# 384 rows of w_down on eight chosen DMA engines, in a decode kernel of cached attention and a SwiGLU block

## The chip, the cores and the metric

The kernel runs on one core of a Trainium2 chip. The metric is the device time of one execution in microseconds; lower is better. A core has a matrix engine (TensorE, PE in the profile), a vector engine (VectorE, DVE), a scalar engine (ScalarE, ACT), a general engine (GpSimd, POOL) and an engine that does little but issue DMAs (SyncE, SP). Sixteen DMA engines, numbered 0 to 15, move data between memory (HBM) and the on-chip buffer (SBUF, 128 partitions). A DMA that an engine issues is cut into shares for some of the sixteen; each DMA engine works off its shares in the order in which one issuing engine queued them.

## The reference

One token goes through an attention block with a long key/value cache and through a gated feed-forward block, and the two results are mixed by a sigmoid gate. With D = 512, 32 query heads, 8 key/value heads, a cache of 32768 rows of 128, and F = 1792:

```python
g = _sigmoid((x * gate_w).sum(-1, keepdims=True))
# A: attention with the cache, then the output matrix
q = (x @ wq).reshape(B, Sq, 32, 128).transpose(0, 2, 1, 3)
k, v = jnp.repeat(k_cache, 4, axis=1), jnp.repeat(v_cache, 4, axis=1)
p = _softmax(jnp.einsum("bhqd,bhkd->bhqk", q, k) * 128 ** -0.5, axis=-1)
a = jnp.einsum("bhqk,bhkd->bhqd", p, v).transpose(0, 2, 1, 3).reshape(B, Sq, 4096) @ wo
# B: feed-forward
b = (_silu(x @ w_gate) * (x @ w_up)) @ w_down
return g * a + (1 - g) * b
```

All tensors are bf16. The two caches are 64 MB each, wq and wo 4 MB each, w_gate, w_up and w_down 1.75 MB each: 148 MB are read for one small row of 512 outputs.

## The kernel before

SBUF holds five pages of 32 KB per partition (`page`, PG_A = 0, PG_B = 1, PG_C = 2, PG_V = 3 and 4). Weights, K and V go through these pages, so a load can be issued only when the page that it fills is free.

**SyncE's queue** sets the order of all large transfers. It issues, one after the other and each behind the wait that frees its page: wq (L335), w_gate and w_up (L337), K of group 0 (two pages, L315), then for each group g the K of g (L315 for g = 1, L306 after that) and the V of g - 1 (L330), the V of the last group, the first 1664 rows of w_down into the tile `wd` (L345), the last 128 rows of w_down (L351), and wo in five chunks (L356), of 16, 9, 4, 2 and 1 rows of each partition's 32.

In the main load of w_down a partition holds FM = 13 consecutive rows (13 KB), and FR = 1664 rows are covered. The other 128 rows go to the first 32 partitions of PG_A, four rows to a partition, in eight DMAs of four partitions each (`wx`). PG_A is free when TensorE has transposed the last K unit (`sem_fill` at UPG * G); wo is put into PG_V, which is free when the V of the group before the last has been used (`sem_v_free`).

**The start of the kernel** computes the queries from wq, then g and u of the feed-forward block. VectorE makes t = silu(g) * u * (1 - gate) as `trow`, four partitions' strips of 448 columns, and spreads it into `tmask` (L706, 1792 columns, each strip masked to its own partition). TensorE turns t into columns with matmuls against a column of ones (L541): 13 for the main rows into `tT`, 4 for the others into `tX` (copies at L713 and L714). Two matmuls then release the loop (L553).

**The loop** goes over the eight groups. TensorE transposes K in 16 units of eight blocks (`emit_fill`, L364, two bf16 at a time as one f32), VectorE copies each unit to SBUF (L735), TensorE multiplies with the queries (L376). Maxima, exponentials (ACT, L619) and sums follow, and the V of the group before is multiplied with its exponentials (L433). The third load of K (g = 2) is issued when half of group 1's units have been transposed.

**The end** (`emit_end`) uses the last V, adds up, and runs the strips of w_down: one matmul for each of `wd`'s 13 columns and four for `wx` (`emit_strip`, L232), all into the four rows of `ps_c`. It then multiplies with wo as chunk after chunk lands (L232 for the first, L243 for the others), and the row of 512 is stored in two halves (L267).

GpSimd fills constants at the start (L275 to L287) and afterwards only passes on semaphores of the K loads. It issues no DMA.

Of the kernel before, what the change touches and what calls it, by code (L numbers as in the profile page):

```python
# [6 lines left out]
ALU = mybir.AluOpType  # L7
# [5 lines left out]
def bass_gated_mix__gqa_block_cached__swiglu_ffn__decode_kernel(  # L13
# [62 lines left out]
    assert G % 2 == 0  # L76
    PAD = 768

    XQ, XE, FX = 8, 4, 4
    XP = XQ * XE  # L80
    FM = FC - XP * FX // 128
    FR = 128 * FM
    assert FR + XP * FX == F and FX == NSTRIP

    with ExitStack() as es:
        def S_(name):
            return es.enter_context(nc.semaphore(name))
# [9 lines left out]
        sem_ld_g = S_("s_ld_g")  # L97
        sem_ld_wd = S_("s_ld_wd")
        sem_ld_wx = S_("s_ld_wx")
        sem_ones = S_("s_ones")  # L100
        sem_dc = S_("s_dc")
        sem_pz = S_("s_pz")
# [59 lines left out]
        qblk = T("qblk", [128, (G + 2) * STEP], BF16)  # L162
        qcur = T("qcur", [128, 2, 2 * HPG], BF16)
        tT = T("tT", [128, FM], BF16)
        tX = T("tX", [XP, FX], BF16)
        pad = T("pad", [128, PAD // 2], BF16)
        page = T("page", [128, NPG, PAGE], BF16)
        wd = T("wd", [128, FM, NOUT], BF16)
# [13 lines left out]
        O2a = T("O2a", [128, WOJ], BF16)  # L182
        O2 = T("O2", [128, WOJ], BF16)
        res_row = T("res_row", [128, 128], BF16)

        def P(name, shape, dt):
            return es.enter_context(nc.psum_tensor(name, shape, dt))
# [34 lines left out]

        wq_v = page[:, PG_Q, 0 : KC * H * DH].rearrange("p (c n) -> p c n", c=KC)
        wgu = page[:, PG_F, 0 : 2 * KC * F].rearrange("p (w c f) -> p w c f", w=2, c=KC)
        wx = page[0:XP, PG_A, 0 : FX * NOUT]
        wx_v = wx.rearrange("p (i n) -> p i n", i=FX)
        wo_v = page[:, PG_X, 0 : WOJ * NOUT].rearrange("p (j n) -> p j n", j=WOJ)
        qall = qblk[:, :].rearrange("p (g e c) -> p g e c", e=2, c=2 * HPG)

# [42 lines left out]
        with nc.Block("main") as block:  # L272
            @block.gpsimd
            def _(pool):
                pool.memset(ones_f[:, :], 1.0).then_inc(sem_ones, 1)  # L275
                pool.memset(ones_bf[:, :], 1.0).then_inc(sem_ones, 1)
                pool.memset(r_row[:, 0, 0:1], 0.0).then_inc(sem_r, 1)
                n, k = 1, 1
                while n < 128:
                    pool.wait_ge(sem_r, k)  # L280
                    pool.tensor_scalar(
                        r_row[:, 0, n : 2 * n], r_row[:, 0, 0:n], float(n), None, op0=ALU.add
                    ).then_inc(sem_r, 1)
                    n *= 2
                    k += 1
                pool.wait_ge(sem_r, k)
                pool.tensor_scalar(  # L287
                    r_row[:, 1, :], r_row[:, 0, :], -1.0, None, op0=ALU.mult
                ).then_inc(sem_r, 1)
                for g in range(1, G):  # L290
                    pool.wait_ge(sem_k[1], 16 * g)
                    if g > 1:
                        pool.wait_ge(sem_k[0], 16 * (g + 1))
                    else:
                        pool.wait_ge(sem_k1, 16)
                    pool.sem_inc(sem_k[1], 16)

            @block.sync
            def _(sp):
                def load_k(g):  # L300
                    lo = PG_A if g % 2 else PG_B
                    dst = page[:, lo : lo + NB, :].rearrange("p b (r d) -> p b r d", d=DH)
                    src = A_k_cache[0, g, :, :].rearrange("(p b r) d -> p b r d", b=NB, r=R)
                    if g > 1:
                        sp.wait_ge(sem_fill, UPG * (g - 1) + UPP)
                        sp.dma_start(  # L306
                            dst.rearrange("p b r d -> p (b r d)"),
                            src.rearrange("p b r d -> p (b r d)"),
                        ).then_inc(sem_k[0], 16)
                        return  # L310
                    for b in range(NB):
                        first = lo + b == PG_B
                        if g and first:
                            sp.wait_ge(sem_fill, UPP)
                        sp.dma_start(dst[:, b, :, :], src[:, b, :, :]).then_inc(  # L315
                            sem_k[0] if first else sem_k1 if g else sem_k[1], 16
                        )

                def load_v(g):
                    src = A_v_cache[0, g, :, :].rearrange("(p b r) d -> p b r d", b=NB, r=R)  # L320
                    if g == G - 1:
                        lo, sem = PG_L, sem_vl
                        sp.wait_ge(sem_fill, UPG * g + UPP)
                    else:
                        lo, sem = PG_V, sem_v
                        if g:
                            sp.wait_ge(sem_v_free, STEP * (g + 1))
                        else:
                            sp.wait_ge(sem_pe_h, 1)
                    sp.dma_start(  # L330
                        page[:, lo : lo + NB, :].rearrange("p b n -> p (b n)"),
                        src.rearrange("p b r d -> p (b r d)"),
                    ).then_inc(sem, 16)

                sp.dma_start(wq_v, A_wq.rearrange("(p c) n -> p c n", c=KC)).then_inc(sem_q, 16)  # L335
                for w, src in enumerate((B_w_gate, B_w_up)):
                    sp.dma_start(  # L337
                        wgu[:, w, :, :], src.rearrange("(p c) f -> p c f", c=KC)
                    ).then_inc(sem_f, 16)
                load_k(0)  # L340
                for g in range(1, G):
                    load_k(g)
                    load_v(g - 1)
                load_v(G - 1)
                sp.dma_start(  # L345
                    wd[:, :, :], B_w_down[0:FR, :].rearrange("(p j) n -> p j n", j=FM)
                ).then_inc(sem_ld_wd, 16)
                sp.wait_ge(sem_fill, UPG * G)
                rest = B_w_down[FR:F, :].rearrange("(e q i) n -> q e (i n)", q=XQ, i=FX)
                for q in range(XQ):  # L350
                    sp.dma_start(wx[q:XP:XQ, :], rest[q]).then_inc(sem_ld_wx, 16)  # L351
                sp.wait_ge(sem_v_free, STEP * G)
                src = A_wo.rearrange("(p j) n -> p j n", j=WOJ)
                for k, s in enumerate(sem_wo):
                    a, b = WO_CUTS[k], WO_CUTS[k + 1]
                    sp.dma_start(wo_v[:, a:b, :], src[:, a:b, :]).then_inc(s, 16)  # L356

            @block.tensor
            def _(pe):
# [103 lines left out]
                def emit_start():  # L463
# [70 lines left out]
                                    skip_group_check=True,  # L534
                                )
                    ins.then_inc(sem_pe_h, 1)
                    pe.wait_ge(sem_dve_tm, 1)
                    for c, n, lo, hi, m in ((M_T0, FM, 0, FR, 128), (M_T0 + FM, FX, FR, F, XP)):
                        tv = tmask[:, lo:hi].rearrange("p (m j) -> p j m", j=n)
                        for j in range(n):  # L540
                            ins = pe.matmul(  # L541
                                ps_m[0:m, c + j : c + j + 1],
                                tv[:, j, :],
                                ones_bf[:, 0:1],
                                start=True,
                                stop=True,
                            )
                    ins.then_inc(sem_pe_t, 1)
                    pe.wait_ge(sem_ps0, 1)
# [20 lines left out]
                def emit_end():  # L570
                    emit_v(
                        [[(sem_exp, (G + 1) * STEP), (sem_vl, 16)], []], (PG_L, PG_L + 1)
                    )
                    pe.wait_ge(sem_rc, G * STEP)
                    emit_reduce((G + 1) * STEP)
                    pe.wait_ge(sem_ld_wd, 16)
                    for j in range(FM):
                        emit_strip(pe, wd, tT, j, j < NSTRIP, False)
                    pe.wait_ge(sem_ld_wx, 16 * XQ)
                    for j in range(FX):  # L580
                        emit_strip(pe, wx_v, tX, j, False, False, at=FM)

                    pe.wait_ge(sem_dve_oT2, 1)
                    pe.matmul(
                        ps_m[:, M_O0 : M_O0 + WOJ], pmat[:, :], O2a[:, :], start=True, stop=True
                    ).then_inc(sem_pe_O2, 1)
                    pe.wait_ge(sem_dve_O2, 1)
                    emit_wo(pe, 0)
# [42 lines left out]
            def _(dve):  # L631
# [43 lines left out]
                for par in range(2):  # L675
# [27 lines left out]
                        ALU.mult,  # L703
                    )
                )
                dve.tensor_tensor(  # L706
                    tmask.rearrange("p (s f) -> p s f", s=NSTRIP),
                    trow.unsqueeze(1).to_broadcast([128, NSTRIP, FS]),
                    strip_sel.unsqueeze(2).to_broadcast([128, NSTRIP, FS]),
                    ALU.mult,  # L710
                ).then_inc(sem_dve_tm, 1)
                dve.wait_ge(sem_pe_t, 1)
                dve.tensor_copy(tT[:, :], ps_m[:, M_T0 : M_T0 + FM]).then_inc(sem_dve_tT, 1)  # L713
                dve.tensor_copy(  # L714
                    tX[:, :], ps_m[0:XP, M_T0 + FM : M_T0 + FM + FX]
                ).then_inc(sem_dve_tT, 1)

                def emit_out(i, at):
# [102 lines left out]
```

## Time and profile before

| what | value |
|---|---|
| median of 3 runs | 350.08 us (349.88 to 350.38) |
| the profiled execution's own time | 349.81 us |
| its span, first to last instruction | 348.5 us |
| bytes read | 148.11 MB, 425 GB/s over the span |
| queue q1 (SyncE's): share of 16 engines' span | 98.7% |
| PE busy | 262.4 us (75%) |
| DVE busy | 186.3 us (53%) |
| ACT busy / POOL busy | 33.4 us (10%) / 2.8 us (1%) |
| main w_down load, issue to landing | 31.3 us |
| wo chunks, issue to landing | 18.4 to 21.7 us |

The span is the time between the first and the last instruction of the core; the execution's time has 1.3 us more around it. In the page's slices a digit is the busy share of one fortieth of the span (8.7 us) in tenths. The chain of waits follows the work that ended last back from the last instruction, at each step to what released it. The timeline lists instructions by their start, with the idle time before them and its cause in brackets. Beside these views the trace holds a record of every DMA packet with its start, its duration, its size and its queue, but not the number of its DMA engine.

### The profile page before, as it was taken

The page shows a single profiled execution, that of the slowest core. Times are in us where ns is not written, and L with a number is a line of the kernel's source. Part 1 is how long each engine was busy: PE and PEld are TensorE (multiplying, and loading weights), DVE is VectorE, ACT ScalarE, POOL GpSimd, SP SyncE. Part 2 cuts the span into 40 slices and gives each one's busy share as a digit, 9 for nine tenths or more (in the row PEclk, how much of TensorE's full clock was granted, in tenths as well). Part 3 has the DMA queues.
Part 4 walks back from the last instruction along what each step waited for, and adds up shares of the span by engine and source line. Part 5 has one row for each costly group of instructions (what it writes and reads, how often), then busy time and mean ns, then how long its engine had stood idle before and what let it go on. Part 6 is the DMA issues. An engine that isn't in the chain of part 4 may idle for free.

```text
span 348.5 us, 8862 instructions
## 1 busy us (share of the span) xinstructions
PE 262.4 (75%) x3921; PEld 222.3 (64%) x3921; DVE 186.3 (53%) x228; ACT 33.4 (10%) x143; POOL 2.8 (1%) x15
## 2 busy tenths in 40 slices
PE   1355996799859981999469992999379973999384
PEld 1125986699459941997269942996279843995241
DVE  4044885499239921697139911895149920894101
ACT  1002000300030003000400003000400012000400
POOL 3000000000000000000000000000000000000000
PEclk9975798699889986799859987998859995898678
DMA  8999999999999999999999999999999999999996
GB/s 311 428 463 421 419 427 466 461 406 436 421 444 451 414 436 421 459 436 414 436 436 451 429 414 436 436 451 429 414 444 451 429 436 414 444 459 414 392 396 266
DMA packets 3970, 148.21 MB, mean 425 GB/s; under 512 B 474, under 2 KB 604, under 8 KB 892
## 3 DMA queue, kind: packets, MB, share of 16 engines
q1 hardware_dynamic: 3956, 148.11, 98.7%
q8 instruction: 6, 0.10, 0.1%
q10 hardware_dynamic: 8, 0.00, 0.0%
HBM read 148.11 MB, written 0.00 MB: 425 GB/s over the span
## 4 chain that ended last, share of the span: by engine, by line
DMA 58%; PE 36%; DVE 3%; issue 2%; SPq 1%; ACT 0%; DVEq 0%
DMA page<-in_A_k_cache_dram 46%; PE pst L364 26%; DMA page<-in_A_wo_dram 6%; PE ps_sc L376 6%; DMA page<-in_B_w_up_dram 6%; PE ps_o L433 2%; DVE ktT L735 1%; PE pst L528 1%; DVE ktT L706 1%; SPq L356 0%; PE ps_m L541 0%; PE ps_m L553 0%; DVE pmaxf L743 0%; DVE ktT L697 0%; PE ps_sc L243 0%
## 5 line engine op out<-in xcount | busy, mean ns | idle before, releaser
L735 DVE COPY ktT<-pst 128x2048 bf16<-128x2048 bf16 x128 | 153.6, 1222 | 65.3 <-PE pst L364 60.9
L364 PE MATMUL pst<-ident_f,page 128*128 128x128 f32 x1024 | 149.7, 302 | 38.4 <-DMA page<-in_A_k_cache_dram 35.4
L364 PEld LDWEIGHTS pst<-ident_f,page 128*128 128x128 f32 x1024 | 128.6, 156 | 42.5 <-DMA page<-in_A_k_cache_dram 35.9
L376 PEld LDWEIGHTS ps_sc<-qcur,ktT 128*128 128x128 bf16 x2048 | 64.0, 97 | 7.9 <-DVE ktT L735 6.8
L376 PE MATMUL ps_sc<-qcur,ktT 128*128 128x8 bf16 x2048 | 64.3, 166 | 6.1 <-DVE ktT L735 6.1
L433 PE MATMUL ps_o<-page,ET 128*16 128x512 bf16 x512 | 38.9, 472 | 5.7 <-DMA page<-in_A_v_cache_dram 5.7
L433 PEld LDWEIGHTS ps_o<-page,ET 128*16 128x16 bf16 x512 | 14.5, 107 | 26.2 <-issue 18.8
L619 ACT ACTIVATE ET<-ps_sc,nbias 128x128 bf16 x64 | 23.9, 555 | 53.3 <-DVE nbias L761 53.3
L612 ACT ACTIVATE acc<-ps_o 128x512 f32<-128x512 f32 x8 | 4.8, 597 | 220.0 <-PE ps_o L433 215.7
L753 DVE TENSOR_REDUCE gm<-ps_m 4x1 f32<-4x128 f32 x8 | 2.2, 279 | 39.3 <-PE ps_m L413 39.3
L619 ACT ACTIVATION_READ_ACCUMULATOR ET<-ps_sc,nbias 128x1 f32 x64 | 18.2, 285 | 0.0
L743 DVE TENSOR_REDUCE pmaxf<-ps_sc 128x4 f32<-128x512 f32 x16 | 11.0, 687 | 8.4 <-PE ps_sc L376 8.4
L490 PE MATMUL pst<-page,xT 128*1 128x512 bf16 x32 | 3.6, 627 | 8.9 <-DMA page<-in_A_wq_dram 8.9
L454 PE MATMUL ps_m<-sel,acc 128*128 128x4 f32 x64 | 8.4, 255 | 1.8 <-ACT acc L612 1.6
L454 PEld LDWEIGHTS ps_m<-sel,acc 128*128 128x128 f32 x64 | 7.7, 191 | 2.5 <-ACT acc L612 2.2
L417 PE MATMUL ps_m<-diag,ones_f 4*128 4x4 f32 x16 | 3.2, 268 | 6.9 <-DVE diag L757 6.9
L720 DVE RECIPROCAL rS<-ps_m 128x4 f32<-128x4 f32 x9 | 1.6, 183 | 12.1 <-PE ps_m L454 12.1
L417 PEld LDWEIGHTS ps_m<-diag,ones_f 4*128 4x128 f32 x16 | 2.7, 213 | 8.4 <-issue 8.4
L490 PEld LDWEIGHTS pst<-page,xT 128*1 128x1 bf16 x32 | 1.0, 115 | 10.7 <-issue 10.7
L670 DVE CAST ktT<-pst 128x1024 bf16<-128x1024 f32 x2 | 2.4, 1220 | 8.4 <-PE pst L490 8.4
L445 PEld LDWEIGHTS ps_m<-esum,ones_f 128*128 128x128 f32 x32 | 4.2, 190 | 3.5 <-issue 3.5
L445 PE MATMUL ps_m<-esum,ones_f 128*128 128x4 f32 x32 | 4.9, 258 | 0.0
(73 smaller groups left out, 49.4 us busy)
## 6 DMA issues: line engine op xcount, KB each, us to landing
page<-in_A_k_cache_dram SPq DMA_DIRECT2D x4, 4096.0 KB, 34.8
page<-in_A_wq_dram SPq DMA_DIRECT2D x1, 4096.0 KB, 13.4
page<-in_A_wo_dram SPq DMA_DIRECT2D x1, 2048.0 KB, 18.4
page<-in_B_w_gate_dram SPq DMA_DIRECT2D x1, 1792.0 KB, 17.1
page<-in_B_w_up_dram SPq DMA_DIRECT2D x1, 1792.0 KB, 20.9
wd<-in_B_w_down_dram SPq DMA_DIRECT2D x1, 1664.0 KB, 31.3
page<-in_A_wo_dram SPq DMA_DIRECT2D x1, 1152.0 KB, 20.8
page<-in_A_wo_dram SPq DMA_DIRECT2D x1, 512.0 KB, 21.5
```

The source lines that it names most:

```text
L364: ins = pe.transpose(pst[u % NST][:, k * 128 : (k + 1) * 128], kv[:, n * 128 : (n + 1) * 128], ident_f[:, :],)
L376: ins = pe.matmul(ps_sc[b][:, col : col + 2 * HPG], kt[:, k, e, :], qcur[:, e, :], start=(e == 0), stop=(e == 1),)
L417: pe.matmul(ps_m[:, M_B0 : M_B0 + HPG], ones_f[0:HPG, :], diag[:, :], start=True, stop=True,).then_inc(sem_b, STEP)
L433: ins = pe.matmul(ps_o[32 * c : 32 * c + RQ * HPG, :], ET[:, n : n + RQ, :].rearrange("p n h -> p (n h)"), v[:, k * RQ : (k + 1) * RQ, :], ...
L445: pe.matmul(ps_m[:, M_S0 : M_S0 + HPG], ones_f[:, :], esum[:, b, :], start=(b == 0), stop=(b == NB - 1),)
L454: ins = pe.matmul(ps_m[:, M_P0 : M_P0 + HPG], acc[:, q, :], sel4[:, q * HPG : (q + 1) * HPG], start=(q == 0), stop=(q == RQ - 1),)
L490: ins = pe.matmul(pst[0][32 * k : 32 * k + 1, t * QN : (t + 1) * QN], xT[:, c : c + 1], wq_v[:, c, n : n + QN], start=(c == 0), stop=(c == ...
L528: ins = pe.matmul(pst[1][32 * k : 32 * k + 1, w * 512 : w * 512 + FS], xT[:, c : c + 1], wgu[:, w, c, k * FS : (k + 1) * FS], start=(c == ...
L612: act.activation(part, ps_o[:, :], ACT.Copy).then_inc(sem_acc, STEP)
L619: act.activation(ET[:, b * R : (b + 1) * R, h], sc[:, h, bass.ds(bank, R)], ACT.Exp, bias=nbias[:, h : h + 1], scale=SCALE, accum_out=esum ...
L735: dve.tensor_copy(ktT[:, n % NKT, :], pst[n % NST][:, :].bitcast(BF16)).then_inc(sem_cp, 1)
L743: dve.tensor_reduce(pmaxf[:, b, :], sc, AX.X, ALU.max).then_inc(sem_d, 1)
```

## The change

The main load has 11 rows to a partition (FM = 11, FR = 1408). The other 384 rows are laid out as two halves (h) of 32 partitions with six rows each, 6 KB. A half is cut into eight shares (e) of four partitions (q). SyncE loads the shares 0 to 4 of both halves in one DMA each, to partitions 0 to 19 and 32 to 51; the first dimension of five is what makes five engines of it. GpSimd loads the shares 5 to 7, to partitions 84 to 95 and 116 to 127. Ahead of each of its two loads it issues a small "spare" load of 13 rows of 64 bytes, so that the loads of three shares go to the three engines after thirteen; after each load it waits for the spare one.

The tile spans all 128 partitions (`wz`), and half of them are not loaded, so GpSimd first clears it (3072 columns), after the wait for PG_A that SyncE had; SyncE now waits for this memset (`sem_wz`). On TensorE the t columns of these rows are made for 64 partitions twice, below and above (11 + 2 x 6 = 23 matmuls at L541 for 17), the strips are 11 and 6 for 13 and 4, and there is a wait for GpSimd's loads (`sem_wp`) besides the one for SyncE's. On VectorE the last 384 columns of `tmask` are written once more in the order (e, q, i), by two instructions behind a wait for the first.

```diff
-    XQ, XE, FX = 8, 4, 4
-    XP = XQ * XE
-    FM = FC - XP * FX // 128
+    XH, XE, XQ, FX = 2, 8, 4, 6
+    XL, XD = 5, 13
+    XP = XE * XQ
+    XS = 2 * XH * XP
+    FM = FC - XH * XP * FX // 128
...
-        wx = page[0:XP, PG_A, 0 : FX * NOUT]
-        wx_v = wx.rearrange("p (i n) -> p i n", i=FX)
+        wz = page[0:XS, PG_A, 0 : FX * NOUT]
+
+        def load_rest(eng, h, lo, hi, sem):
+            at = 64 * (lo > 0) + 32 * h
+            rest = B_w_down[FR:F, :].rearrange(
+                "(h q e i) n -> h e q (i n)", h=XH, q=XQ, e=XE
+            )
+            eng.dma_start(wz[at + XQ * lo : at + XQ * hi, :], rest[h, lo:hi]).then_inc(sem, 16)
...
+                pool.wait_ge(sem_fill, UPG * G)
+                pool.memset(wz, 0.0).then_inc(sem_wz, 1)
+                pool.wait_ge(sem_wz, 1)
+                for h in range(XH):
+                    pool.dma_start(spare[:, :], A_wq[0:XD, 0:32]).then_inc(sem_sp, 16)
+                    load_rest(pool, h, XL, XE, sem_wp)
+                    pool.wait_ge(sem_sp, 16 * (h + 1))
...
-                sp.wait_ge(sem_fill, UPG * G)
-                rest = B_w_down[FR:F, :].rearrange("(e q i) n -> q e (i n)", q=XQ, i=FX)
-                for q in range(XQ):
-                    sp.dma_start(wx[q:XP:XQ, :], rest[q]).then_inc(sem_ld_wx, 16)
+                sp.wait_ge(sem_wz, 1)
+                for h in range(XH):
+                    load_rest(sp, h, 0, XL, sem_ld_wx)
...
-                    pe.wait_ge(sem_dve_tm, 1)
...
+                    pe.wait_ge(sem_dve_tm, XH)
...
+                    cols = [(tv[:, j, :], 128) for j in range(FM)]
+                    cols += [(tx[:, i, :], XH * XP) for i in range(FX)]
+                    for j, (lhsT, m) in enumerate(cols):
+                        for lo in range(0, 128, m):
                             ins = pe.matmul(
-                                ps_m[0:m, c + j : c + j + 1],
-                                tv[:, j, :],
+                                ps_m[lo : lo + m, M_T0 + j : M_T0 + j + 1],
+                                lhsT,
...
-                    pe.wait_ge(sem_ld_wx, 16 * XQ)
+                    pe.wait_ge(sem_ld_wx, 16 * XH)
+                    pe.wait_ge(sem_wp, 16 * XH)
...
+                n = XP * FX
+                for h in range(XH):
+                    lo = F - n * (XH - h)
+                    at = FS - n * (XH - h)
+                    dve.tensor_scalar(
+                        tmask[:, lo : lo + n].rearrange("p (e q i) -> p e q i", e=XE, q=XQ),
+                        trow[:, at : at + n].rearrange("p (q e i) -> p e q i", e=XE, q=XQ),
+                        strip_sel[:, NSTRIP - 1 : NSTRIP],
+                        None,
+                        op0=ALU.mult,
+                    ).then_inc(sem_dve_tm, 1)
```

More of the change, by code (lines that the diff above doesn't have):

```diff
@@ L77, in bass_gated_mix__gqa_block_cached__swiglu_ffn__decode_kernel @@
     PAD = 768
-    XQ, XE, FX = 8, 4, 4
-    XP = XQ * XE
-    FM = FC - XP * FX // 128
+    XH, XE, XQ, FX = 2, 8, 4, 6
[3 more added lines that the diff above has]
+    FM = FC - XH * XP * FX // 128
     FR = 128 * FM
-    assert FR + XP * FX == F and FX == NSTRIP
+    assert FR + XH * XP * FX == F and XS == 128
+    assert XH * XP * FX <= FS and XL + 8 == XD and XD + XE - XL == 16
     with ExitStack() as es:
@@ L99, in bass_gated_mix__gqa_block_cached__swiglu_ffn__decode_kernel @@
         sem_ld_wx = S_("s_ld_wx")
+        sem_wz = S_("s_wz")
+        sem_wp = S_("s_wp")
+        sem_sp = S_("s_sp")
         sem_ones = S_("s_ones")
@@ L164, in bass_gated_mix__gqa_block_cached__swiglu_ffn__decode_kernel @@
         tT = T("tT", [128, FM], BF16)
-        tX = T("tX", [XP, FX], BF16)
+        tX = T("tX", [XS, FX], BF16)
         pad = T("pad", [128, PAD // 2], BF16)
@@ L184, in bass_gated_mix__gqa_block_cached__swiglu_ffn__decode_kernel @@
         res_row = T("res_row", [128, 128], BF16)
+        spare = T("spare", [XD, 32], BF16)
         def P(name, shape, dt):
@@ L536, in emit_start @@
                     ins.then_inc(sem_pe_h, 1)
-                    pe.wait_ge(sem_dve_tm, 1)
-                    for c, n, lo, hi, m in ((M_T0, FM, 0, FR, 128), (M_T0 + FM, FX, FR, F, XP)):
-                        tv = tmask[:, lo:hi].rearrange("p (m j) -> p j m", j=n)
-                        for j in range(n):
+                    pe.wait_ge(sem_dve_tm, XH)
+                    tv = tmask[:, 0:FR].rearrange("p (m j) -> p j m", j=FM)
+                    tx = tmask[:, FR:F].rearrange(
+                        "p (m i) -> p i m", i=FX
+                    )
+                    cols = [(tv[:, j, :], 128) for j in range(FM)]
+                    cols += [(tx[:, i, :], XH * XP) for i in range(FX)]
+                    for j, (lhsT, m) in enumerate(cols):
+                        for lo in range(0, 128, m):
                             ins = pe.matmul(
-                                ps_m[0:m, c + j : c + j + 1],
-                                tv[:, j, :],
+                                ps_m[lo : lo + m, M_T0 + j : M_T0 + j + 1],
+                                lhsT,
                                 ones_bf[:, 0:1],
@@ L546, in emit_start @@
                                 stop=True,
+                                skip_group_check=True,
                             )
@@ L578, in emit_end @@
                         emit_strip(pe, wd, tT, j, j < NSTRIP, False)
-                    pe.wait_ge(sem_ld_wx, 16 * XQ)
+                    pe.wait_ge(sem_ld_wx, 16 * XH)
+                    pe.wait_ge(sem_wp, 16 * XH)
+                    w = wz.rearrange("p (i n) -> p i n", i=FX)
                     for j in range(FX):
-                        emit_strip(pe, wx_v, tX, j, False, False, at=FM)
+                        emit_strip(pe, w, tX, j, False, False, at=FM)
                     pe.wait_ge(sem_dve_oT2, 1)
@@ L705, in _ @@
                 )
[L706 to L711, printed above, removed]
+                dchain(
+                    dve.tensor_tensor(
+                        tmask.rearrange("p (s f) -> p s f", s=NSTRIP),
+                        trow.unsqueeze(1).to_broadcast([128, NSTRIP, FS]),
+                        strip_sel.unsqueeze(2).to_broadcast([128, NSTRIP, FS]),
+                        ALU.mult,
+                    )
+                )
+                n = XP * FX
[9 more added lines that the diff above has]
+                    ).then_inc(sem_dve_tm, 1)
                 dve.wait_ge(sem_pe_t, 1)
@@ L714, in _ @@
                 dve.tensor_copy(
-                    tX[:, :], ps_m[0:XP, M_T0 + FM : M_T0 + FM + FX]
+                    tX[:, :], ps_m[:, M_T0 + FM : M_T0 + FM + FX]
                 ).then_inc(sem_dve_tT, 1)
```

## The prediction

> **What bounds the kernel now.** I read the page's slices first, then the chain of waits in order of time, then SyncE's timeline, then the single DMA packets in the trace. The slices:
>
> ```profile
> DMA  8999999999999999999999999999999999999996
> GB/s 311 428 463 421 419 427 466 461 406 436 421 444 451 414 436 421 459 436 414 436 436 451 429 414 436 436 451 429 414 444 451 429 436 414 444 459 414 392 396 266
> ```
>
> The DMA engines are busy from the second slice to the last but one. The end of the chain:
>
> ```profile
> 324.47 21.67 DMA page<-in_A_wo_dram
> 346.14 0.04 issue
> 346.18 0.64 PE ps_sc L243 x12
> ...
> 346.84 0.29 DVE res_row L788
> ```
>
> wo is issued at 324 and its last chunk lands at 346.14; 2.4 us later the span ends. So the end is the end of the slowest of 16 DMA queues, and what SyncE issued before wo lies in the same queues:
>
> ```profile
> 305.42 0.43 SPq L345 DMA_DIRECT2D wd<-in_B_w_down_dram  x1
> 315.34 5.07 SPq L351 DMA_DIRECT2D page<-in_B_w_down_dram  x8
> 323.14 2.24 SPq L356 DMA_DIRECT2D page<-in_A_wo_dram  x5
> ```
>
> In the packet records a packet starts where its engine's last one ended, so the engines can be followed singly, though not by number. Packets step at 2.414 us (64 KB), 0.607 (16 KB), 0.494 (13 KB), 0.344 (9 KB) and 0.161 (4 KB with its completion). Nine engines begin the main w_down load at 329.98 to 330.50, seven at 330.96 to 331.65. The page counts six packets of instruction code; the one at 35.49 took 0.89 us, and its engine's next K packet 1.76 instead of 1.21: 1.4 us, about the lateness, and a seventh engine has such a loss without a record at 79. The four engines with the eight 4 KB packets (L351) are among the early ones. Their wo ends at 345.85 to 346.07, the seven late ones' at 345.84 to 346.08, the other five early ones' at 344.57 to 345.12. Between 334.9 and 336.7 packets of all sizes run slower (16 KB: 1.0 us), which costs each engine some 0.6 us. I find no cause for that stretch in the trace.
>
> **The bytes.** wo alone takes 8 x (0.607 + 0.344 + 0.155 + 0.080 + 0.042) = 9.85 us per engine. Before, without the slow stretch: a late engine 331.65 + 8 x 0.494 + 9.85 = 345.45, one with extra rows 330.37 + 3.95 + 1.29 + 9.85 = 345.46; seen 346.08, so the stretch is 0.6. After: the main load is 88 KB instead of 104 per engine; between the 9 and 13 KB packets, an 11 KB one is 0.419, eight 3.35. A late engine: 331.65 + 3.35 + 9.85 = 344.85, 0.6 earlier. Engines 0 to 3 keep 136 KB: eight 6 KB packets at about 0.23 are 1.85, so 330.37 + 3.35 + 1.85 + 9.85 = 345.42, unchanged. The four new ones (4, 13 to 15) rise from 104 to 136 KB; if they are early ones, at most 330.50 + 5.20 + 9.85 = 345.55. So 32 KB more on the early engines, which is what their lead is worth, become 48 KB, and the end is theirs: 345.55 against 345.46, or +0.1 us, if the stretch still costs 0.6.
>
> **SyncE and GpSimd.** L351's eight issues (0.63 us each) become two, behind a wait for GpSimd's memset of 3072 columns. No row has that memset; bounds from these two and from the 1x64 and 1x128 TENSOR_SCALAR (0.36, 0.53):
>
> ```profile
> 0.74 0.20 POOL L275 MEMSET ones_f<- 128x128 f32 x1 [0.29 <-POOLq L806]
> 0.88 0.10 POOL L276 MEMSET ones_bf<- 128x2 bf16 x1
> ```
>
> They give 0.86 ns a column, 2.7 us; by the other slope 8.4. I take 2.7, a memset's. Queued behind the wait on SyncE are the two loads and wo's five issues, which wait for L356 at 323.14 anyhow: 315.3 + 2.7 + 1.3 = 319.3. With 8.4 wo would be issued at 325, still eight us before an engine comes to it. Cost nothing.
>
> GpSimd's DMAs have no row. The nearest is a small load beside a full queue:
>
> ```profile
> 1.30 0.22 ACTq L599 DMA_DIRECT2D gw_row<-in_gate_w_dram  x1
> 8.08 0.68 DVE L663 TENSOR_TENSOR gp_row<-x_row,gw_row 1x512 f32<-1x512 bf16 x1 [1.82 <-DMA gw_row<-in_gate_w_dram]
> ```
>
> Its 1 KB packet ran at 6.39, some four 32 KB packets after its issue, and its completion one 1.21 us packet later. At 64 KB a packet the first spare load then has its data near 318.6 + 4 x 2.4 = 328, its completion near 331; the second pair goes behind 11 KB packets and lands near 336. PE reads these rows at L232 at 340.0 and next waits for wo at 341.7: four us of cover; later than about 342 each us is lost in full. What a change of queue costs an engine is bounded by gw_row's turn (the neighbouring packets kept 1.21: nothing) and the code packet's (0.27 + 0.55 us over its bytes). I take nothing, gw_row's turn being a plain load into the same memory, and keep 0.8 a turn.
>
> Where do these loads go? The eight before, of four rows each, ran on four engines, one 4 KB packet apiece, so an engine takes a whole share of rows; by this GpSimd's three shares of four rows are three engines' work, 24 KB each and load. [...]
>
> **The start.** The changed steps there lie on the chain that leads, without a wait for DMA, to the issue of the third K load:
>
> ```profile
> 27.86 2.04 DVE ktT L706
> ...
> 29.94 1.18 PE ps_m L541 x17
> ...
> 31.23 0.15 DVE tX L714
> ...
> 31.52 0.98 PE ps_m L553 x4
> 32.50 5.31 PE pst L364 x24
> ...
> 76.42 23.80 DMA page<-in_A_k_cache_dram
> ```
>
> Added: two TENSOR_SCALARs of 192 columns at about 0.27 (the 128-column rows take 0.23 to 0.29), the wait between (0.05), and 23 matmuls instead of 17 at L541, 6 x 0.07. Together 1.0 us, so that load would be issued at 77.4. The first engines finish V at 78.62, and from an issue to a first packet it took 1.05 us at the start (0.74 to 1.79; two engines 0.5 and 1.0 later). So 14 engines are served in time by 0.1 us, one or two may idle 0.5. Bounds 0 and 1.2 (PE's stalls for code at 48.2 and 54.4, 0.5 and 1.7 us, may shift too); I take 0.2, nearer to nothing since only the earliest engines have no slack. At the end PE still has 11 + 6 = 13 + 4 strips: nothing.
>
> **Sum.** Profiled execution 349.81 (span 348.5): +0.1 for the bytes, +0.2 for the start, 350.1. The median of the runs is 0.27 above the profile: 350.4. Own range 349.8 to 350.9.
>
> **Rivals.**
> - *The slow stretch goes* (0.17). It falls where 4 KB packets, w_down and wo mix, and the eight strided loads are gone. For it: no other change of load shows it. Against: w_down and wo still mix. The end is then 345.55 instead of 346.08: 349.6, or 349.8 with the start's 0.2.
> - *Each change of queue costs as the code packet did* (0.19). Two loads on 13 to 15 and two spares on 0 to 12, at least two turns of 0.8 each: +1.6, so 352.0; five turns for each load (four rows and a completion) would be +8. It decides from 0.4 us a turn on. Against: gw_row's turn.
> - *The third K load comes too late* (0.13). Issued 2.2 us later instead of 1.0, it lets the nine early engines idle for up to 1.2, and their lead, on which the 48 KB are laid, is gone: +1.2, 351.5. It decides from about 1.2 us of delay.
> - *The engines meant are not the early ones* (0.07): a late engine with 136 KB ends at 346.08 + 1.25, 351.3. Against: 0 to 3 are early, and a run of late ones from 5 on would fit.
> - *GpSimd's rows spread, one row to an engine* (0.04): 12 engines with 6 KB from each load, 13 to 15 with nothing; 0 to 4 then carry 148 KB and end 2 x 0.23 later, 350.9. [...]
> - *GpSimd's loads land after 342* (0.05): +1 or more, 351.5.
>
> **Chances.** The forecast has 0.35. 0.2% is 0.7 us, about what a measurement of this kernel can tell from no change. Faster by more: 0.15, over half of the first rival (its 0.5 can be more if the timed runs have a larger lead than the profile) and a little of the forecast. Slower by more: 0.46, the other five rivals (0.48) without their milder outcomes. Within: 0.39. The range leaves out the deepest gains and the five-turn case: 349.4 to 352.2.
>
> **What would show it.** Right: the last wo packets of eight engines near 346.1, of the other eight near 345.5; L541 with 23 matmuls and the third K load issued near 77.4, with no gap in the packets at 79; GpSimd's rows landed before 340. Wrong: no slow packets at 335; K or V packets longer than 2.42 us next to GpSimd's; 6 KB packets on late engines; a wait for w_down rows on PE ahead of L232.

## The result, and the profile after

The changed kernel takes 351.49 us (median of 6 runs, 351.25 to 351.93) against 349.97 for the kernel before in the same runs: slower by 1.5 us, ratio 1.0044 (95% interval 1.0033 to 1.0055). That lies in the stated range, on the side that had the larger chance, but 1.1 us above the likeliest time and above the forecast's own range, which ended at 350.9.

The end of the chain of waits, after:

```profile
346.34 2.38 PE ps_sc L257 x72
...
348.74 0.29 DVE res_row L829
```

The last copy (L788 before, L829 now) starts at 348.74 instead of 346.84, 1.9 us later; this profiled execution took 351.71, 0.2 more than the median. The chain shows TensorE's 72 matmuls there, but by the packet records wo's last packets still end the work: they end at 347.95, where they ended at 346.08 before, and the copy follows 0.8 us later both times.

SyncE's timeline and GpSimd's, after:

```profile
74.23 0.33 SPq L327 DMA_DIRECT2D page<-in_A_k_cache_dram  x1
...
305.95 0.44 SPq L366 DMA_DIRECT2D wd<-in_B_w_down_dram  x1
318.60 1.68 SPq L239 DMA_DIRECT2D page<-in_B_w_down_dram  x2
321.99 2.24 SPq L376 DMA_DIRECT2D page<-in_A_wo_dram  x5
```

```profile
315.92 2.66 POOL L312 MEMSET page<- 128x3072 bf16 x1 [311.90 <-PE pst L384]
318.88 0.70 POOL L315 DMA_DIRECT2D spare<-in_A_wq_dram  x1 [0.31 <-POOL page L312]
319.58 0.58 POOL L239 DMA_DIRECT2D page<-in_B_w_down_dram  x1
327.63 0.52 POOL L315 DMA_DIRECT2D spare<-in_A_wq_dram  x1 [7.47 <-DMA spare<-in_A_wq_dram]
328.19 0.56 POOL L239 DMA_DIRECT2D page<-in_B_w_down_dram  x1
```

Nothing here is late: the memset took 2.66 us, wo was issued earlier than before (321.99 for 323.14), and the third K load came 2.2 us earlier, not 1.0 later. So the loss is in the DMA queues, between 329 and 339. The windows view shows it (the last two columns are the DMA engines' busy share and GB/s); first before, then after:

```profile
332.00:336.00 4.00, 3.90 (x44) 1.55 (x48) 0.00 (x0) 0.00 (x0) 0.00 (x0) 0.56 1.05 385
336.00:340.00 4.00, 3.78 (x53) 2.20 (x45) 0.54 (x3) 0.60 (x1) 0.00 (x0) 1.00 0.97 409
```

```profile
332.00:336.00 4.00, 2.83 (x28) 1.08 (x32) 0.00 (x0) 0.00 (x0) 0.00 (x0) 0.50 1.06 343
336.00:340.00 4.00, 3.77 (x50) 2.12 (x43) 0.00 (x0) 0.60 (x1) 0.00 (x0) 0.91 1.00 402
```

The engines are fully busy in both, and move less after the change. I add up, over all packets of SyncE's queue from 300 on, how much longer each took than is usual for its size. Before this is 10.3 engine-us (us of one engine, summed over the sixteen), between 334.4 and 337.1; after it is 25.9, between 329 and 338.6. That is 1.6 us for each of the sixteen engines instead of 0.64. This is what the text calls the slow stretch, or the stretch.

The packet records also show where GpSimd's 24 packets of 6 KB lay, on queue q0 of its own. The records carry no engine numbers; the five engines with SyncE's 6 KB packets are called 0 to 4 here, as in the prediction, and the numbers stand for nothing more. GpSimd's first load lay on three of these; its second on the other two of them and on one engine that begins the main load late. So engines 0 to 4 had 24 KB more than the change meant (4 packets of 0.234 us, 0.94 us), and the three that got no packet of the first 13-row spare, called 13 to 15, got none of the rows. Engines 0 to 4 ended at 347.82 to 347.96, the late one at 347.72, the three at 345.80 to 346.00.

### The profile page after: what moved, and what is told of

Its sections match the earlier page's. It is cut to its first block, busy times and chain, and to the rows that moved or that the text cites. A ratio compares the mean times of both kernels' runs of the same rounds, so it can differ in the third digit from the quotient of the medians.

```text
span 350.4 us, 8877 instructions
## 1 busy us (share of the span) xinstructions
PE 261.1 (75%) x3927; PEld 220.9 (63%) x3927; DVE 186.6 (53%) x230; ACT 33.4 (10%) x143; POOL 7.8 (2%) x20
## 5 line engine op out<-in xcount | busy, mean ns | idle before, releaser
L384 PE MATMUL pst<-ident_f,page 128*128 128x128 f32 x1024 | 147.0, 299 | 38.1 <-DMA page<-in_A_k_cache_dram 36.3
L384 PEld LDWEIGHTS pst<-ident_f,page 128*128 128x128 f32 x1024 | 126.1, 154 | 42.3 <-DMA page<-in_A_k_cache_dram 36.8
L312 POOL MEMSET page<- 128x3072 bf16 x1 | 2.7, 2657 | 311.9 <-PE pst L384 311.9
```

The lines of the kernel that those rows point to most:

```text
L384: ins = pe.transpose(pst[u % NST][:, k * 128 : (k + 1) * 128], kv[:, n * 128 : (n + 1) * 128], ident_f[:, :],)
```

## The experiments

Two theories were to be told apart first. A: GpSimd's loads lay on 0 to 2 and 3 to 5, because the spare did not move the cursor, as the place is called here from which GpSimd's next DMA would take its engines (a supposition of the author's: the records show only where packets lay). B: GpSimd's queue as such slows all engines. The runs then raised a third question, what the slow stretch is.

**A spare of 26 rows** in 13 groups of two that cannot be merged, a pattern of the same kind as that of the loads behind it (the tile `spare` has 26 rows, too):

```diff
-pool.dma_start(spare[:, :], A_wq[0:XD, 0:32])
+pool.dma_start(spare[:, :], A_wq[0 : 2 * XD, 0:32].rearrange("(b a) c -> a b c", a=XD))
```

> The changed kernel, but each spare load has 26 rows in 13 groups of two, in a pattern of the same kind as the loads behind it (groups that cannot be merged into one run of rows). Theory A (in the changed kernel GpSimd's two loads lay on engines 0 to 2 and 3 to 5, because the 13-row spare did not move the cursor: 24 KB more on each of 0 to 4, 0.9 us of the 1.5; the rest is a longer slow stretch): the spare now moves the cursor, the 6 KB packets of GpSimd's queue lie on three engines without SyncE's extra rows, both times the same three, and the time falls by 0.9 us or more, to 350.2 to 350.7. Rival B (GpSimd's queue itself, its turns and completions, slows all engines): no change within 0.2 us, 351.3 to 351.7, wherever the packets lie.

The twelve times fall into two groups: five at 348.98 to 349.22, seven at 350.49 to 350.76. The profile is of the lower group (348.98). There GpSimd's packets lie on three engines without SyncE's rows, both loads on the same three, and not one packet is slow (0.04 engine-us over the usual):

```profile
332.00:336.00 4.00, 3.74 (x36) 1.36 (x40) 0.00 (x0) 0.00 (x0) 0.00 (x0) 0.50 1.03 432
```

432 GB/s where the changed kernel has 343. The engines of 136 KB end at 345.11 to 345.34, the prediction's sum without a stretch was 345.42 to 345.55. So in this group A holds for the placement, and B falls: four DMAs from GpSimd, with as many packets as in the changed kernel (224), cost nothing, and none of the twelve runs is as slow as B wanted. But the gain was larger than the 0.9 us of the bytes, since the stretch went too.

**No spares at all**: the two spare loads and the waits for them taken out.

> The changed kernel without the two spare loads and the waits for them. Theory A: the spares did not steer, so GpSimd's 6 KB packets lie on engines with SyncE's extra rows as before, and the time stays at 351.3 to 351.7. Rival B: half of GpSimd's DMAs and their completions are gone, so about half of the 1.5 us comes back, 350.6 to 350.9. If the spares did steer, the loads now go elsewhere and the time changes by about 0.9 us or more.

351.44 us (351.28 to 351.71), as the changed kernel. GpSimd's first load lies on three of SyncE's five engines, its second on the other two and a late one, and the stretch is 25.5 engine-us. So the 13-row spares, which the change had put there to lead the loads to the three engines after thirteen, steered nothing. B, which wanted half of the loss back, falls again.

**No extra rows**: the kernel before with 14 row blocks in the main load.

```diff
-    FM = FC - XP * FX // 128
+    FM, FX = FC, 0
```

(with the extra load, its columns and strips taken out)

> The kernel before with all 14 row blocks in the main load and no extra rows at all, 112 KB on every engine. Asks what the slow stretch near the end hangs on. By the packet steps without a stretch: late engines end at 331.65 + 4.24 + 9.85 = 345.7, early ones at 344.6. Theory A1 (the stretch comes with the 4 or 6 KB packets of extra rows, written or read in their pattern): no slow packets between 330 and 338, last wo packet near 345.7, time 349.6, 0.35 below the kernel before. Rival B1 (the stretch comes with w_down's and wo's reading as such): it costs 0.6 us as before, last wo packet near 346.35, time 350.25.

350.63 us (350.40 to 351.00), ratio to before 1.0018 (1.0010 to 1.0027). There was no slow stretch, as A1 says, but the time was 1.0 above A1's. The lead of the early engines was gone. SyncE's timeline:

```profile
78.53 0.33 SPq L303 DMA_DIRECT2D page<-in_A_k_cache_dram  x1
```

The third K load was issued at 78.53; in the chain TensorE stood 3.6 us at 61.3 on "issue", and between 78 and 80 the DMA engines idled for 5.1 engine-us, nearly all of it on the early ones. The ten packets with which these began again took 3.0 to 3.5 us instead of 2.42, 8.1 engine-us in all, so idling is the smaller part: the two together are 0.8 us for each engine. All sixteen then ended V between 331.85 and 333.00. Why even the last of them is 1.35 us later than the last one before (331.65) stays open, and the profiled run was the slowest of the eleven. The prediction's rival of the late third K load is thus a real mechanism, here in another kernel, and the kernel before has little room: 76.42 in its trace.

**256 extra rows**, four to a partition, with the 26-row spares:

```diff
-    XH, XE, XQ, FX = 2, 8, 4, 6
+    XH, XE, XQ, FX = 2, 8, 4, 4
```

> As the kernel with the 26-row spares, but 256 extra rows, four to a partition: 12 row blocks in the main load (96 KB per engine) and 32 KB more on eight engines. If the spares steer (theory A) and the stretch costs 0.6 us: late engines 331.65 + 3.65 + 9.85 + 0.6 = 345.75, early ones at most 330.5 + 3.65 + 1.27 + 9.85 + 0.6 = 345.87, against 346.08 before: 349.75, 0.2 below the kernel before. With a stretch of 1.5 us as in the changed kernel 350.7. Rival B: above 351.0 as long as GpSimd has four DMAs.

Again unlike times: three at 348.88 to 349.05, the rest at 349.88 to 350.51, 0.9998 of before in all (0.9990 to 1.0007). The profile is of the lower group; no slow packets, wo's last packet at 345.26.

So the stretch is there where 4 or 6 KB rows are loaded in one way and not where they are loaded in another. What differs is which engine writes which partitions. In a load over 128 partitions each engine writes eight of them (eight 13 KB packets on each engine in the main load before), but no packet record names a partition, so no run shows which eight. The changed kernel's layout gives each engine four partitions of a half; these are called its own here, which is a name and no finding. In the kernel before engine e (0 to 3) wrote its extra rows to partitions 8e to 8e + 7. In the changed kernel GpSimd's rows were laid for engines 13 to 15 and, by A, went to 0 to 5. Theory C is that the stretch comes from engines that write extra rows into partitions which others write in a full load. That the layout's partitions are free of this was the author's supposition. The theory is tested by moving rows and nothing else.

**Own partitions, SyncE alone**: the kernel before with its 128 rows eight to a partition, in four loads of 8 KB rows instead of eight of 4 KB, so that engine e writes 4e to 4e + 3. X0 is the first of the 16 partitions (the places where it is used are left out).

```diff
-    XQ, XE, FX = 8, 4, 4
+    XQ, XE, FX, X0 = 4, 4, 8, 0
```

> [...] Four loads instead of eight, 32 KB more on engines 0 to 3 as before. Theory C (the slow stretch comes from engines that write into the partitions of other engines): no slow packets between 333 and 338, last wo packet near 345.45 instead of 346.08, time 349.3 to 349.5, 0.6 below the kernel before. Rival B1 (the stretch comes with reading w_down and wo side by side): unchanged within 0.2, 349.8 to 350.1.

349.14 us (348.86 to 349.27), ratio 0.9975 (0.9966 to 0.9984): faster than both kernels. No packet is slow (0.05 engine-us). The end of its chain and the window:

```profile
323.12 22.21 DMA page<-in_A_wo_dram
345.33 0.04 issue
...
346.00 0.29 DVE res_row L791
```

```profile
332.00:336.00 4.00, 4.00 (x40) 1.53 (x44) 0.00 (x0) 0.00 (x0) 0.00 (x0) 0.50 1.04 442
```

The sum without a stretch was 345.45; the last packet ended at 345.40.

**Partitions 64 to 79, SyncE alone**: the same kernel with X0 = 64, so that the same four engines write the same bytes to partitions 64 to 79.

> [...] Theory C: the slow stretch is there, at least as long as in the kernel before (10 engine-us over the unhindered packet times) and 0.6 us or more above the kernel with its own partitions: 349.9 to 351. Rival B1: equal to the kernel with its own partitions within 0.2.

351.22 us (350.23 to 352.35), 2.1 us above the kernel with own partitions and more than C's 349.9 to 351, with 31.1 engine-us of stretch:

```profile
332.00:336.00 4.00, 3.93 (x40) 1.54 (x44) 0.00 (x0) 0.00 (x0) 0.00 (x0) 0.50 1.10 369
336.00:340.00 4.00, 3.78 (x44) 2.13 (x35) 0.00 (x0) 0.60 (x1) 0.00 (x0) 0.82 0.99 369
```

The two kernels differ in one constant, so for SyncE's loads the partitions decide, as C foretold, and B1 falls; why they do is not shown. 128 KB are written so, and all engines lose 1.9 to 2.0 us, not only the four that write. What sets the size is open: the 128 KB of the kernel before, in partitions 0 to 31, cost a third of it (10.3 engine-us).

**The 26-row spares again**, with no other kernel beside it that issues DMAs from GpSimd:

> The kernel with the 26-row spares once more, now without another kernel beside it that issues DMAs from GpSimd. It had two groups of times, 349.0 to 349.2 and 350.5 to 350.8, and its profiled run was one of the first, with GpSimd's rows on the three engines meant and no slow packet. Theory D (the cursor of GpSimd's DMAs outlives a run, and the kernel beside it, which moves it by 6, set it elsewhere): one group only, all near 349.1 or all near 350.6. Rival E (something within the kernel's own run decides): both groups again, in about the same shares.

Both groups again: six runs at 349.10 to 349.36, six at 350.30 to 350.76. D falls: the two groups need no other kernel. The profile was of the lower group once more, with both loads on three engines without SyncE's rows.

**SyncE's half alone**: the changed kernel without GpSimd's loads and spares; 144 rows of w_down are left out of the result.

> The changed kernel without GpSimd's loads and spares: the shares 5 to 7 of both halves (144 rows of w_down) are left out of the result, the memset stays. SyncE's 48 KB on each of engines 0 to 4 go into own partitions. Theory C: no slow packets, engines 0 to 4 end last, near 330.4 + 3.35 + 1.85 + 9.85 = 345.4, time 349.0 to 349.3; so SyncE's half of the change costs nothing and GpSimd's half all of it. Rival F (the 11-row main load, the later start or SyncE's wait for the memset cost a part): above 349.6.

348.90 us (348.76 to 349.08). Engines 0 to 4 end at 345.16 to 345.40, and the stretch is 0.6 engine-us. The 11-row main load, the later start, the memset and SyncE's 240 rows together cost nothing; all that the change loses, 2.6 us against this kernel, is in GpSimd's 144 rows.

**GpSimd's rows in other partitions**: the 26-row spares, and the rows of 13 to 15 in partitions 20 to 31 and 52 to 63.

```diff
-            at = 64 * (lo > 0) + 32 * h
+            at = 32 * h
```

> [...] Bytes, engines and queues as in the kernel with 26-row spares, whose undisturbed times are 349.0 to 349.4. Theory C: the slow stretch is there (over 5 engine-us), the first profiled run is at 349.8 or more, and no run is below 349.5. Rival B (a foreign partition costs nothing when it is GpSimd that loads): the same two groups, the lower again near 349.1.

350.72 us in the profiled run and 351.77 to 352.13 in the others; none in the lower range. 25.6 engine-us of stretch against 0.04 with partitions 84 to 95 and 116 to 127, and 354 GB/s where that kernel had 432:

```profile
332.00:336.00 4.00, 2.85 (x28) 1.06 (x32) 0.00 (x0) 0.00 (x0) 0.00 (x0) 0.50 1.04 354
```

In the profile both loads lie on the same three engines, without SyncE's rows, as there. The partitions decide for GpSimd's loads too.

**The spares without the rows** (144 rows left out again):

> The kernel with 26-row spares, with the two spare loads and their waits but without GpSimd's loads of rows (144 rows of w_down are left out of the result, as in the kernel with SyncE's loads alone, 348.8 to 349.1). Asks where the upper group of times of the 26-row kernel (350.3 to 350.8, beside 349.0 to 349.4) is from. Theory G (the spares, which also write into partitions of other engines, set off the slow stretch in some runs): two groups again, 348.9 and 350 or more. Rival H (it is the rows: in some runs the cursor stands elsewhere and the 48 KB go to other engines and foreign partitions): one group, 348.8 to 349.1.

349.02 us, one group (348.76 to 349.54). So the 26-row spares, 128 bytes for each engine, set off nothing (0.04 engine-us), and the upper group of the 26-row kernel comes from the rows. That in those runs the rows went to other engines than those for which they were laid could make the 1.2 to 1.5 us; but no profile fell into that group, so it is argued, not shown, and what would move them from run to run is open.

## Why the prediction was right or wrong

- **The bound and the sum: right.** The end is the end of the slowest DMA queue. Where nothing else disturbed, the packet steps gave the ends to 0.1 to 0.3 us: 345.45 predicted without a stretch and 345.40 measured with partitions 0 to 15, 345.42 to 345.55 and 345.11 to 345.34 with the 26-row spares. One reading was off and changed nothing: of the seven late engines before, the one that began at 330.96 ended at 345.39, not with the others.
- **The range and the chances: held, in part by luck.** Of the 0.48 that the five slower rivals had, only the 0.07 for wrong engines was on what came; the turns of the queue (0.19), the late K load (0.13) and the late landing (0.05) did not happen in this kernel.
- **The step that failed first: where GpSimd's loads go.** "If they are early ones" carried the forecast, and the share rule drawn from SyncE's loads was taken to hold for the spares. The rows did go in whole shares of three engines, but from engine 0 on, as the engines are numbered here. The 13-row spare lay with one row on each of 13 engines, and the loads behind it went where they go without any spare, so it steered nothing. That the spares lead the loads to 13 to 15, on which the sum's 136 KB for these three rest, no run shows: no record numbers an engine, and the changed kernel's rows lay on the five engines with SyncE's and on a late one. The rival for this case had 0.07 and a price of +1.25 for a late engine with 136 KB; what came was 160 KB on 0 to 4, +0.94 over the forecast.
- **The term that was mis-sized: the slow stretch.** It was kept at 0.6 us, for want of a cause in one trace; on the engines 0 to 4, which ended last, it was 1.5. The rival that it goes had its mechanism half right (the strided loads make it) and wrong in what matters (not their size or mix, but the partitions). It was gone with partitions 0 to 15 (0.05 engine-us). With 0.94 for the bytes and 0.9 for the longer stretch, the 1.87 us between the last packets are accounted for to 0.1 us.
- **The start: the sizes right, the effect wrong.** The two TENSOR_SCALARs took 0.45 us in all (0.54 predicted) and the 23 matmuls 1.42:

```profile
30.16 0.45 DVE L746 TENSOR_SCALAR ktT<-ktT,ident 128x192 bf16<-128x192 bf16 x2
...
30.67 1.42 PE L566 MATMUL ps_m<-ones_bf,ktT 128*128 128x1 bf16 x23 [4.64 <-DVE ktT L746]
```

  The loop began 0.9 us later, but its first 24 matmuls took 4.38 us instead of 5.38 (the granted clock from 33 to 40 was 0.76 for 0.60), and 16 others 1.96 for 3.38, behind a wait of 1.61 instead of 2.40; so the third K load was issued at 74.23. Why the clock was granted earlier the trace does not show. The 0.2 us of the sum was nothing.
- **The change of queue: the choice right, the rival refuted.** Until 329, a 64 KB packet of V behind one of GpSimd's 64-byte, 4-byte or 6 KB packets took the usual 2.418 us; the first of GpSimd's 6 KB packets took 0.234. Six V packets that began at 329.1 to 329.4 took 2.9; with the 26-row spares, where GpSimd's packets are as many, none did, so these belong to the stretch.
- **The memset, SyncE's wait and GpSimd's landing: right.** 2.66 us for 2.7; SyncE's loads issued at 318.6 and wo not late; GpSimd's last packet at 337.75, 1.7 us later than predicted and 3 us before PE's strips.

## What to carry to other kernels

Before rows are moved to chosen DMA engines, look in the packet records whether the present odd-shaped loads make all packets slow, and lay the same rows in other partitions: here partitions 0 to 15 instead of 0 to 31, with four loads of SyncE's instead of eight, gave 0.8 us, while the elaborate balance lost 1.5. A load that is to steer where the next one goes may not do so: here one of another pattern kind did not, and with one of the same kind half of the runs were still slow. Its effect must be seen in the records. A lead of some engines over others is worth its bytes only as long as no load is issued so late that the early ones idle, as the kernel without extra rows shows.

## What the runs showed of the hardware

- Here it hung on which engines wrote the extra rows into which partitions whether all sixteen DMA engines slowed down. 128 KB from four engines cost 0.05 engine-us with partitions 0 to 15, 31.1 with 64 to 79, and 10.3 with 0 to 31 in the kernel before. 144 KB from GpSimd, on three engines without SyncE's rows, cost 0.04 with 84 to 95 and 116 to 127 and 25.6 with 20 to 31 and 52 to 63; with 84 to 95 and 116 to 127 from the five engines with SyncE's rows and a late one, as in the changed kernel, 25.9; the 26-row spares alone, 128 bytes for an engine, 0.04. No run here shows the mechanism, only that all queues slow down together: 1.9 to 2.0 us for each engine with 64 to 79.
- The packet of instruction code at 35.49 in the kernel before cost its DMA engine 1.4 us (0.89 for its 16 KB and 0.55 more on the next packet). Six are on record in every kernel, and with own partitions six engines began the main load at 331.22 to 331.58, the other ten at 329.83 to 330.28: these packets very likely make the late engines, though only one was followed.
- GpSimd's DMAs waited long behind full queues: the first spare was issued at 318.88 and landed 8.5 us later, its packets on one engine some 2.4 us apart, a 64 KB packet between them.
